# Attention block on one core: first x block in two transfers and four pieces, first K and Q from unpadded weights, first score tiles by head pairs, some bound rows on GpSimd

## The chip, the cores and the metric

The kernel runs on one core of one Trainium2 chip. The metric is device time in microseconds (us), the median of three runs. A core has a matrix engine (TensorE, here PE, with its weight loads shown apart as PEld), a vector engine (VectorE, DVE), an engine for functions such as the exponential (ScalarE, ACT), a programmable one (GpSimd, POOL) and an engine that issues transfers (SyncE, SP). Each takes its own instructions in the order in which the program lists them and waits on semaphores for what others have to finish. Matmul results go to PSUM, everything else lives in SBUF, and 16 DMA engines move data between these and DRAM.

## The reference

One attention block in bfloat16: a sequence of 2048 rows of 448 columns, 16 heads of 28 columns each. The scale is 28 to the power of -1/2.

```python
def reference(x, wqkv, wo):
    B, S, D = x.shape                      # 1, 2048, 448
    H = 16
    Dh = D // H                            # 28
    qkv = (x @ wqkv).reshape(B, S, 3, H, Dh).transpose(2, 0, 3, 1, 4)
    q, k, v = qkv[0], qkv[1], qkv[2]
    scores = jnp.einsum("bhqd,bhkd->bhqk", q, k) * (Dh ** -0.5)
    p = softmax(scores, axis=-1)
    o = jnp.einsum("bhqk,bhkd->bhqd", p, v)
    return o.transpose(0, 2, 1, 3).reshape(B, S, D) @ wo
```

## The kernel before

**Tiling.** The 16 heads are taken in four groups of four (G, HG), the 2048 queries in four chunks of 512 (QW), the 2048 keys in 16 tiles of 128. A window is one group with one chunk of queries; there are 16. A score tile is 128 keys by 512 queries of one head, 1024 in all: one matmul (L874) into a PSUM bank. A head has 28 columns and is padded to 32 partitions (HP), so four heads lie side by side on 128 partitions. Two heads share a 64-row matmul operand: KB[.][0] and QB[.][0] serve heads 0 and 1 of a group, KB[.][1] and QB[.][1] heads 2 and 3.

**Softmax with a bound.** In place of a row maximum an upper bound of each score is subtracted by the score matmul itself. Of the 64 rows of an operand, 32 carry a head's K or Q, and the other 32 carry bound rows: on the Q side the absolute values of Q times the K maxima (L681 to L691), on the K side a negative constant. For key block 0 and the first two windows the constants come from bndcol in the eviction (L547). For key blocks 1 to 3 they are the ratio of the maximum over all keys (KMAX, L580) to that over block 0 (RK0, L545), written into NK (L585) and copied out by DMA (L600). Four to eight DMAs (L590) move K itself to its place.

**Exponentials.** Most score tiles go in pairs through a two-bank PSUM slot (PA) to ACT (L1294, 128x1024). The others go one at a time through PD: DVE and POOL compute the exponential from a polynomial in the bits (L1075, L1078, L1081, L1094), and a few tiles do it almost wholly on POOL (L1007 to L1037). The value matmuls (L1139) add up four heads at once in PO.

**Order.** All of it stands in one function. The code first lists operations with an engine, an assumed duration, dependencies and a priority (class Op, add), then runs a small event simulation of the five engines (L1339 to L1392) and emits the instructions in the order that this simulation chose. The numbers in the operations are assumptions that decide an order; on the chip each engine just follows that order and the semaphores. A changed assumption such as XLAT, the assumed landing times of the x blocks, can therefore reorder the whole program.

**The start.** SP issues the first x block, the Q weights, two more x blocks and the V weights (L281 to L288), then four transposing loads of the last x block (L291). ACT issues the K weights (L280) and loads its function table (L297). PE runs eight filler matmuls on zeros (L404), then transposes x block 0 in two halves of eight (L425). DVE evicts the first half and half of the second, ACT the other (L436, L438). The weights of the first group are copied into padded form by DVE and ACT (L389, L390). K and Q of block 0 are four matmuls each with 112 rows per step (L531, L661). ACT evicts Q (L675) and K twice (L547), DVE reduces K's maximum (L538), forms the bound rows (L681 to L687) and evicts the later x blocks, with ACT taking one half (L438). Then the first scores follow.

**Order of the first score tiles.** `tile_of` maps the running number of a tile to its window, key tile and head. Within a row of four tiles all heads of one key tile come first:

```python
def tile_of(n):
    k, i = divmod(n, HG)
    w, j = row_of(k)
    g, c = divmod(w, NQC)
    return w, g, c, j, i
```

The first two windows run over the first four key tiles (FB) each, before the rest of either.

Of the kernel before, what the change touches and what calls it, by code (L numbers as in the profile page):

```python
# [9 lines left out]
ACT = mybir.ActivationFunctionType  # L10
ALU = mybir.AluOpType
# [7 lines left out]
P = 128  # L19
# [65 lines left out]
def kernel(  # L85
# [91 lines left out]
    XLAT = (4.6, 7.3, 8.9, 9.6)  # L177
# [11 lines left out]
    WQE = 'ACT'  # L189
    QORD = 0  # L190
    KCH = ((1, 2), (2, 4))
    RCH = ((1, 4), (0, 1))
# [3 lines left out]
    HENG = ('ACT', 'ACT', 'DVE', 'DVE')  # L196
# [188 lines left out]
    def pad_w(W, WP, g, eng):  # L385
        o = WP[g][:].rearrange("p c (h e) -> p c h e", e=HP)[:, :, :, 0:Dh]
        i = W[:, :, g * GW:(g + 1) * GW].rearrange("p c (h d) -> p c h d", d=Dh)
        if eng == "DVE":
            return lambda: nc.vector.tensor_copy(out=o, in_=i)  # L389
        return lambda: nc.scalar.copy(out=o, in_=i)  # L390
# [3 lines left out]
    xsp = []  # L394
# [3 lines left out]
    tbank = (((PD[0][:], None), (PD[1][:], None)), ((PD[2][:], None), (PA[0][:, 0:QW], None)),  # L398
             ((PO[:], None), (PD[1][:], -2)), ((PD[2][:], 2), (PO[:], 3)))
# [10 lines left out]
    for b in range(NQC - XBAR):  # L410
        xs_in = add(Op("SP", 0.01, None, prio=-2000 + b, lat=XLAT[b]))
        for hf in range(2):
            tv = tbank[b][hf][0].bitcast(BF16)

            if b == 0 and hf == 1 and XSP:
                tv2 = PA[0][:, QW:2 * QW].bitcast(BF16)
            else:
                tv2 = tv
# [8 lines left out]
            tro = add(Op("PE", 0.55 if b else (0.75, 0.65)[hf], tr, deps=[xs_in], prio=(-1200 if b else -5000) + 10 * b + (hf ^ THF[b]), lat=PLAT, kind="T",  # L427
                         elig=None if 2 * b + hf < 2 + TE else lambda t: len(k0mm) == 2 * CC and all(o.end is not None for o in k0mm),
# [10 lines left out]
            if b == 0 and hf == 1 and XSP:  # L439
                evo = add(Op("ACT", 0.48, lambda ev=ev: ev(eng="ACT", c1=1), deps=[tro], prio=-4999))  # L440
                xt_done[b].append(evo)
                evo = add(Op("DVE", 0.36, lambda ev=ev: ev(eng="DVE", c0=1), deps=[tro], prio=-4999))
                xsp.append(evo)
            else:
                evo = add(Op(eng, 0.655 if eng == "DVE" else 0.905, ev, deps=[tro], prio=(EVP[b] if b else -5000) + 10 * b + hf,
                             elig=None if b == 0 or eng == 'ACT' or not BW[b] else lambda t, b=b: len(qb0) == HG and qb0[BW[b] - 1].end is not None))
# [28 lines left out]
    for (W, WP, nm, win) in ((WK, WKP, "k", wkin), (WQ, WQP, "q", wqin)):  # L475
        eng = "DVE" if nm == "k" else WQE
        w_ready[(nm, 0)] = add(Op(eng, 0.3 if eng == "DVE" else 0.45, pad_w(W, WP, 0, eng), deps=[win], prio=-5001 + (nm == "q") * 2.5))
# [27 lines left out]
    def chain_mm(n, fn, deps, prio, elig, acq, half=None):  # L505
        ops = []
        for k in range(n):
            o = add(Op("PE", MM, (lambda k=k: fn(k)), deps=deps if k == 0 else [ops[-1]] + (half if half and k == 2 else []),
                       prio=prio + (0.001 if half is None else 10) * k, kind="B",
                       elig=elig, acq=acq if k == 0 else None, lat=0.0 if k < n - 1 else PLAT))  # L510
            ops.append(o)
        return ops

    k0_bank = [PD[0][:], PD[0][:], PD[1][:], PO[:]]
    k0_wait = [lambda: [xt_half[0]], lambda: kuse[0], lambda: [xt_half[5]], lambda: [xt_half[4]]]

    def task_K(g, sc):
# [11 lines left out]
        def ap():  # L529
            return task["ap"] if "ap" in task else bank(task)[:]  # L530
        ops = chain_mm(CC, lambda cc: nc.tensor.matmul(out=ap(), lhsT=WKP[g][:, cc, :], rhs=XT[sc][cc // 2][0:CK, cc % 2, :],  # L531
                                                       start=(cc == 0), stop=(cc == CC - 1)),
                       (xt_done[sc] if g or sc else xt_done[0][:1]) + [w_ready[("k", g)]], prio, elig, acq, half=None if g or sc else xt_done[0][1:])
        if g == 0 and sc == 0:
            k0mm.extend(ops)
        cs = slice(sc * QW, (sc + 1) * QW)
# [39 lines left out]
    def task_kmax(g):  # L576
# [7 lines left out]
        if g == 0:  # L584
            nk = add(Op("DVE", 0.2, lambda: nc.vector.tensor_scalar(  # L585
                out=NK[0][:], in0=maskm[:, 0:P], scalar1=KMAX[0][:, 0:1], scalar2=RK0[:, 0:1], op0=ALU.mult, op1=ALU.mult),
                deps=[m] + rk_op, prio=prio + 0.2))
# [48 lines left out]
    def task_Q(g, c):  # L636
# [4 lines left out]
        if w == 0:  # L641
            task = {"slot": d_slots[1]}
            acq = lambda t: xt_half[1].done(t)
            elig = None
            prio = -4500
        else:
# [9 lines left out]
            elif w == NF:  # L656
# [4 lines left out]
        ops = chain_mm(CC, lambda cc: nc.tensor.matmul(out=ap(), lhsT=WQP[g][:, cc, :], rhs=XT[c][cc // 2][0:CK, cc % 2, :],  # L661
                                                       start=(cc == 0), stop=(cc == CC - 1)),
                       (xt_done[c] if w else xt_done[0][:1]) + [w_ready[("q", g)]], prio, elig, acq, half=None if w else xt_done[0][1:])
# [8 lines left out]
        if w < NF:  # L672
            pq = -4390 if w == 0 else Q1P - 900
            if w == 0:
                e0 = add(Op("ACT", 0.62, lambda: nc.scalar.activation(  # L675
                    out=qb[0][:], in_=ap(), func=ACT.Identity, bias=offscol[:, 0:1], scale=YSC), deps=[ops[-1]], prio=pq, lat=0.17))
                quse.extend([e0])
# [5 lines left out]
            e1 = add(Op("DVE", TS5, lambda: nc.vector.tensor_copy(out=qb[1][:], in_=qb[0][:]), deps=[e0], prio=pq + 15))  # L683

            def bound(q, i, col, deps, prio):
                st = SI[i]
                return add(Op("DVE", 0.36, lambda: nc.vector.tensor_scalar(  # L687
                    out=q[i // 2][HP * (st ^ 1):HP * ((st ^ 1) + 1), :], in0=QP[n][HP * st:HP * (st + 1), :],
                    scalar1=col[HP * st:HP * (st + 1), 0:1], scalar2=None, op0=ALU.mult), deps=deps, prio=prio))
            for i in range(HG):  # L690
                o = bound(qb, i, KPART[0], [ab, kmaxop[0][0], e1], pq + (20 if i < 2 else 40) + 0.01 * i)  # L691
# [74 lines left out]
    open_when(a_slots[0], [xt_half[3]])  # L766
    a_slots[1].free_at = 0.0
# [97 lines left out]
    def tile_of(n):  # L865
        k, i = divmod(n, HG)
        w, j = row_of(k)
# [595 lines left out]
```

## Time and profile before

| what | value |
|---|---|
| three runs | 410.1, 410.3, 410.46 us |
| median | 410.3 us |
| profiled execution, its own time | 410.69 us |
| its span in the profile | 408.5 us |
| granted TensorE clock, mean | 1.00 |
| ACT, exponentials (L1294) | 422 of them, 388.0 us summed |
| first exponential starts, last one ends | 11.35 and 400.45 us |
| DMA in the first 10 us | 16 to 310 GB/s in steps of 2 us |

A line of a timeline gives the start, the duration from the first start to the last end, the engine, the source line, the operation, output and inputs with shapes, and how many were merged. In square brackets stands how long the engine was idle before it, and what released it. A line of groups gives the summed time, the mean of one in ns, and the idle time before. Consecutive instructions of an engine overlap a little, so that sums of durations can exceed the time that passed.

### The profile page before, as it was taken

To read this page: it belongs to the slowest core of one execution; us is meant where nothing else is said; L and a number is where in the kernel's file an instruction comes from. 1 tells how busy PE (TensorE), PEld (TensorE's weight loads), DVE (VectorE), ACT (ScalarE), POOL (GpSimd) and SP (SyncE) were. 2 spreads that over 40 slices of the span, in tenths; PEclk is the share of its full clock that TensorE was granted. 3 is DMA by queue.
4 is the path that set the end of the run, shared out by engine and by line. 5 is a ranking of instruction groups with operands and counts; after the bars stand their busy time and mean duration, and the time that the engine had idled before them with its cause. 6 is when DMAs were issued, how large, how long until landed. Compare 5 with 4: busy or idle time off the path is not lost.

```text
span 408.5 us, 7585 instructions
## 1 busy us (share of the span) xinstructions
PE 358.8 (88%) x2595; PEld 120.7 (30%) x2606; DVE 380.7 (93%) x664; ACT 395.5 (97%) x434; POOL 341.0 (83%) x365
## 2 busy tenths in 40 slices
PE   8999988998888989888897989889788888889896
PEld 5343232322223232322322232232222222222222
DVE  5996999999899999999989999999989999998983
ACT  4999999999999999999999999999999999999994
POOL 5049998899898999989899998979979989989950
PEclk9999999999999999999999999999999999999999
DMA  9353031112301020200500001000330001010121
GB/s 208 56 85 81 3 57 43 19 47 52 61 3 53 19 41 19 43 2 10 127 18 30 22 7 47 4 30 21 67 64 6 26 11 42 2 52 2 45 103 66
DMA packets 36871, 17.30 MB, mean 42 GB/s; under 512 B 29217, under 2 KB 33569, under 8 KB 36833
## 3 DMA queue, kind: packets, MB, share of 16 engines
q1 hardware_dynamic: 36224, 16.61, 17.8%
q8 instruction: 20, 0.33, 0.3%
q10 hardware_dynamic: 608, 0.22, 0.2%
q14 instruction: 19, 0.15, 0.1%
HBM read 6.91 MB, written 2.33 MB: 23 GB/s over the span
## 4 chain that ended last, share of the span: by engine, by line
ACT 43%; DVE 34%; PE 10%; issue 6%; POOL 4%; DMA 1%; DVEq 0%; SPq 0%; POOLq 0%; ACTq 0%
ACT PTA L1294 43%; DVE DU L1075 8%; DVE DV L1078 8%; DVE PTD L1094 8%; PE PA L874 3%; PE PO L1139 3%; POOL DG L1081 2%; DVE KB L566 1%; DVE SG L1007 1%; PE PD L874 1%; DVE KPART L570 1%; DVE VA L748 1%; DMA RRB<-SCR 1%; PE PA L404 1%; DVE DRC L968 1%
## 5 line engine op out<-in xcount | busy, mean ns | idle before, releaser
L1294 ACT ACTIVATE PTA<-PA 128x1024 bf16<-128x1024 f32 x422 | 388.0, 1175 | 0.9 <-PE PA L874 0.4
L1081 POOL TENSOR_TENSOR DG<-DV,DU 128x512 f16<-128x512 f16 x155 | 177.4, 1154 | 34.2 <-DVE DV L1078 29.8
L874 PE MATMUL PA<-QB,KB 64*128 64x512 bf16 x843 | 169.1, 380 | 36.4 <-ACT PTA L1294 33.6
L874 PEld LDWEIGHTS <-KB 64*128 64x128 bf16 x1024 | 65.4, 93 | 177.9 <-issue 169.3
L1094 DVE SCALAR_TENSOR_TENSOR PTD<-PD,DG 128x512 uint16<-128x512 f32 x155 | 104.7, 682 | 8.2 <-POOL DG L1081 7.8
L1075 DVE TENSOR_SCALAR DU<-PD 128x512 f16<-128x512 uint16 x155 | 103.6, 681 | 5.1 <-PE PD L874 4.8
L1078 DVE SCALAR_TENSOR_TENSOR DV<-PD,DU 128x512 f16<-128x512 uint16 x155 | 103.6, 682 | 0.8
L1139 PE MATMUL PO<-PTA,VA 128*32 128x512 bf16 x843 | 85.5, 386 | 0.7 <-DVE QB L671 0.4
L874 PE MATMUL PD<-QB,KB 64*128 64x512 bf16 x181 | 66.3, 377 | 5.0 <-DVE PTD L1094 3.3
L1139 PE MATMUL PO<-PTD,VA 128*32 128x512 bf16 x181 | 55.6, 386 | 0.3
L1139 PEld LDWEIGHTS <-VA 128*32 128x32 bf16 x1024 | 19.9, 94 | 50.0 <-issue 48.7
L1024 POOL TENSOR_TENSOR SG<-SG,GU 128x512 f32<-128x512 f32 x26 | 30.0, 1156 | 3.0 <-DVE QP L700 2.1
L1022 POOL TENSOR_TENSOR GU<-GV,GU 128x512 f16<-128x512 f16 x26 | 30.0, 1155 | 2.0 <-DVE QP L700 1.4
L1020 POOL TENSOR_TENSOR GV<-GE,GU 128x512 f16<-128x512 f32 x26 | 30.1, 1157 | 1.4
L974 POOL TENSOR_TENSOR OT<-OSB,RRB 128x512 bf16<-128x512 f32 x15 | 19.0, 1269 | 5.2 <-DMA RRB<-SCR 3.7
L1014 POOL TENSOR_SCALAR GU<-SG 128x512 f16<-128x512 uint16 x26 | 16.1, 617 | 5.5 <-DVE SG L1007 3.1
L1007 DVE COPY SG<-PD 128x512 f32<-128x512 f32 x26 | 17.8, 683 | 2.2 <-PE PD L874 2.0
L661 PE MATMUL PO<-XT,WQP 112*128 112x512 bf16 x56 | 18.7, 386 | 0.5 <-DVE KB L558 0.4
L1017 POOL TENSOR_SCALAR GE<-SG 128x512 f32<-128x512 uint16 x26 | 16.1, 618 | 2.9 <-DVE QP L700 1.0
L1037 POOL TENSOR_SCALAR PTD<-SG 128x512 uint16<-128x512 f32 x26 | 16.1, 619 | 1.9 <-DVE KPART L570 0.5
L732 PEld LDWEIGHTS <-XT 112*128 112x128 bf16 x256 | 13.6, 98 | 10.5 <-issue 10.2
L531 PE MATMUL PO<-XT,WKP 112*128 112x512 bf16 x48 | 15.5, 385 | 0.4 <-DVE OSB L959 0.4
(109 smaller groups left out, 201.7 us busy)
## 6 DMA issues: line engine op xcount, KB each, us to landing
RRB<-SCR SPq DMA_DIRECT2D x15, 256.0 KB, 3.3
QB<-QP SPq DMA_DIRECT2D x56, 32.0 KB, 1.8
KB<-NK SPq DMA_DIRECT2D x12, 128.0 KB, 3.0
XS<-in_x_dram SPq DMA_DIRECT2D x3, 448.0 KB, 5.8
QB<-QB SPq DMA_DIRECT2D x28, 32.0 KB, 1.8
out_dram<-XS SPq DMA_DIRECT2D x2, 448.0 KB, 2.5
KB<-KB SPq DMA_DIRECT2D x6, 128.0 KB, 2.3
RRB<-RR SPq DMA_DIRECT2D x2, 256.0 KB, 3.4
```

What stands on the lines that cost most here:

```text
L874: nc.tensor.matmul(out=ap, lhsT=KB[g % 2][i // 2][a:a + 64, j * P:(j + 1) * P], rhs=QB[w % NQB][i // 2][a:a + 64, :], start=True, stop=Tru ...
L974: o5 = add(Op("POOL", 1.22, lambda: nc.gpsimd.tensor_tensor(out=OT[g][c][:], in0=OSB[b][:], in1=RRB[b][:], op=ALU.mult), deps=o4, prio=-10 ...
L1007: cp = add(Op("DVE", CPY, lambda: nc.vector.tensor_copy(out=X[:], in_=PX[slot.idx][:]), deps=[sop], prio=n - O1))
L1020: g3 = add(Op("POOL", PTT, lambda: nc.gpsimd.tensor_tensor(out=GV[:], in0=GE[:], in1=GU[:], op=ALU.mult), deps=[g2], prio=prio + 2, kind=" ...
L1022: g4 = add(Op("POOL", PTT, lambda: nc.gpsimd.tensor_tensor(out=GU[:], in0=GV[:], in1=GU[:], op=ALU.mult), deps=[g3], prio=prio + 3, kind=" ...
L1024: g5 = add(Op("POOL", PST, lambda: nc.gpsimd.tensor_tensor(out=X[:], in0=X[:], in1=GU[:], op=ALU.add), deps=[g4], prio=prio + 4, kind="g", ...
L1075: p1 = add(Op("DVE", P1, lambda: nc.vector.tensor_scalar(out=DU[b][:], in0=lo, scalar1=SIG / 65536, scalar2=SIG * (SS - 0.5), op0=ALU.mult ...
L1078: p2 = add(Op("DVE", P1, lambda: nc.vector.scalar_tensor_tensor(out=DV[b][:], in0=lo, scalar=65536 * (SS - 0.5 + CE / C3), in1=DU[b][:], o ...
L1081: gq = add(Op("POOL", PTT, lambda: nc.gpsimd.tensor_tensor(out=DG[b][:], in0=DV[b][:], in1=DU[b][:], op=ALU.mult), deps=[p2], prio=n, kind ...
L1094: f = add(Op("DVE", P1, lambda: nc.vector.scalar_tensor_tensor(out=PTD[st["s"].idx][:].bitcast(U16), in0=PX[slot.idx][:], scalar=EBITS + C ...
L1139: nc.tensor.matmul(out=PO[HP * st:HP * (st + 1), :], lhsT=VA[g][:, j, st, :], rhs=r["p"][i][1](), start=first, stop=last, tile_position=(0 ...
L1294: nc.scalar.activation(out=PTA[pslot.idx][:, 0:len(ns) * QW], in_=PA[s.idx][:, 0:len(ns) * QW], func=ACT.Exp, bias=ACT_BIAS, scale=ACT_SCALE)
```

## The change

- **First x block.** It is loaded as two transfers of 224 KB, one on SP's queue and one on ACT's, behind the K weights. Its 16 transposes come as two groups of eight, one for each transfer, into four banks (t0_bank); each of the four pieces of 112 columns is evicted by itself, ACT and DVE in turn.
- **First K and Q.** For group 0 and block 0 the matmuls read WK and WQ as they were loaded: one matmul for each head and step, 28 columns wide, at its own column position (strips_mm), into a bank that a matmul of zeros cleared. Q comes before K at each step. The padded copies, which the later blocks read, are made on POOL.
- **Evictions.** ACT evicts Q of window 0 twice in place of a DVE copy. The second half of x block 1 goes from ACT to DVE.
- **Bound rows.** For heads 2 and 3 of the first two windows, and for key block 1, POOL computes the bound rows; the DMAs from NK then cover key blocks 2 and 3 only. RK0 is multiplied by KMAX in an instruction of its own.
- **Score order.** In the first two windows eight tiles of heads 0 and 1 (four key tiles) come before the eight of heads 2 and 3.
- **Fillers.** Four filler matmuls in place of eight, and the twelve optional ones between 4.6 and 9 us of the simulation are gone.
- **Order.** Assumed times and priorities are changed, so the order of instructions differs from the start on. In the built program 844 score tiles go to ACT (843 before) in 422 instructions, all of them full (before, one of the 422 held a single tile); 25 tiles (26) take the way that is almost wholly POOL's.

```diff
-    XLAT = (4.6, 7.3, 8.9, 9.6)
+    XLAT = (None, 6.5, 8.8, 9.6)
...
+    NWARM = 4
+    XLAT0 = (4.0, 4.8)
...
-    RCH = ((1, 4), (0, 1))
+    RCH = ((2, 4), (0, 1))
...
-    HENG = ('ACT', 'ACT', 'DVE', 'DVE')
+    HENG = ('ACT', 'DVE', 'DVE', 'DVE')
...
-        if b < NQC - 1:
+        if b == 0:
+            for h, q in ((0, nc.sync), (1, nc.scalar)):
+                ts = slice(h * TPC // 2, (h + 1) * TPC // 2)
+                q.dma_start(out=XS[0][:, ts, :], in_=x_perm[:, ts, :])
+        elif b < NQC - 1:
...
+        return lambda: nc.gpsimd.tensor_copy(out=o, in_=i)
...
-    for n in range(8):
+    for n in range(NWARM):
...
-    for n in range(12):
-        add(Op("PE", MM, lambda: warm(n), prio=5000, kind="K", elig=lambda t: 4.6 < t < 9, acq=lambda t: warm_open[0]))
...
+    xt0 = []
+    t0_bank = (PO[:], PA[1][:, 0:QW], PA[0][:, 0:QW], PA[0][:, QW:2 * QW])
...
+    for h in range(2):
+        for cc in range(CC):
+            def tr(h=h, cc=cc):
+                for t in range(h * TPC // 2, (h + 1) * TPC // 2):
+                    nc.tensor.transpose(out=t0_bank[cc].bitcast(BF16)[0:CK, t * P:(t + 1) * P],
+                                        in_=XS[0][:, t, cc * CK:(cc + 1) * CK], identity=ident[:])
...
+    for cc in range(CC):
+        eng = ("ACT", "DVE")[cc % 2]
+
+        def ev0(cc=cc, eng=eng):
+            (nc.scalar.copy if eng == "ACT" else nc.vector.tensor_copy)(
+                out=XT[0][cc // 2][:, cc % 2, :], in_=t0_bank[cc].bitcast(BF16)[0:CK, 0:QW])
...
+    def strips_mm(bank, W, win, prio):
+        ops = []
+
+        def clear():
+            nc.tensor.matmul(out=bank, lhsT=zeros[:], rhs=zrow[:], start=True, stop=False, skip_group_check=True)
+        z = add(Op("PE", 2 * MM, clear, deps=[z_in], prio=-5100, kind="K", lat=0.0))
+        for cc in range(CC):
+            def mm(cc=cc):
+                for h in range(HG):
+                    nc.tensor.matmul(out=bank[HP * h:HP * h + Dh, :], lhsT=W[:, cc, h * Dh:(h + 1) * Dh], rhs=XT[0][cc // 2][0:CK, cc % 2, :],
+                                     start=False, stop=(cc == CC - 1), tile_position=(0, HP * h), skip_group_check=True)
...
+            kr = add(Op("DVE", 0.07, lambda: nc.vector.tensor_scalar(
+                out=RK0[:], in0=KMAX[0][:], scalar1=RK0[:, 0:1], scalar2=None, op0=ALU.mult), deps=[m] + rk_op, prio=prio + 0.2))
+            for i in range(HG):
+                def rows0(i=i):
+                    st = SI[i]
+                    nc.gpsimd.tensor_scalar(out=KB[0][i // 2][HP * (st ^ 1):HP * ((st ^ 1) + 1), QW:2 * QW], in0=maskm[HP * st:HP * (st + 1), :],
+                                            scalar1=RK0[HP * st:HP * (st + 1), 0:1], scalar2=0.0, op0=ALU.mult, op1=ALU.add)
...
+                e1 = add(Op("ACT", 0.62, lambda: nc.scalar.activation(
+                    out=qb[1][:], in_=ap(), func=ACT.Identity, bias=offscol[:, 0:1], scale=YSC), deps=[ops[-1]], prio=pq + 15, lat=0.17))
...
+                if i < 2:
+                    return add(Op("DVE", 0.36, lambda: nc.vector.tensor_scalar(out=o, in0=q, scalar1=km, scalar2=None, op0=ALU.mult), deps=deps, prio=prio))
+                return add(Op("POOL", 0.6, lambda: nc.gpsimd.tensor_scalar(out=o, in0=q, scalar1=km, scalar2=0.0, op0=ALU.mult, op1=ALU.add),
+                              deps=deps, prio=prio))
...
+        if k < FB * NF:
+            k, r = divmod(n, FB * HG)
+            k, i = k * FB + r % (2 * FB) // 2, r // (2 * FB) * 2 + r % 2
```

More of the change, by code (lines that the diff above doesn't have):

```diff
@@ L413 @@
             tv = tbank[b][hf][0].bitcast(BF16)
[L415 to L418, printed above, removed]
+            tv2 = tv
             def tr(b=b, hf=hf, tv=tv, tv2=tv2):
@@ L438, in ev @@
                     nc.scalar.copy(out=XT[b][hf][:, c0:c1, :], in_=i)
[L439 to L446, printed above, removed]
+            evo = add(Op(eng, 0.655 if eng == "DVE" else 0.905, ev, deps=[tro], prio=EVP[b] + 10 * b + hf,
+                         elig=None if eng == 'ACT' or not BW[b] else lambda t, b=b: len(qb0) == HG and qb0[BW[b] - 1].end is not None))
             xt_done[b].append(evo)
@@ L765 @@
     task_Q(0, 0)
-    open_when(a_slots[0], [xt_half[3]])
-    a_slots[1].free_at = 0.0
+    for s in a_slots:
+        s.free_at = 0.0
     open_when(d_slots[0], kuse[1])
```

74 lines of the change are left out of this document (40 added, 34 removed).

## The prediction

> **What bounds the kernel now.** I read the engine totals and the costliest groups first, then the timelines of the first 22 us and of the last 15 us, since the diff touches the start and what the new order leaves at the end.
>
> ```profile
> PE 358.8 (88%) x2595; PEld 120.7 (30%) x2606; DVE 380.7 (93%) x664; ACT 395.5 (97%) x434; POOL 341.0 (83%) x365
> ...
> L1294 ACT ACTIVATE PTA<-PA 128x1024 bf16<-128x1024 f32 x422 | 388.0, 1175 | 0.9 <-PE PA L874 0.4
> ```
>
> ACT is busy 97% of the span, and in its 422 exponentials it waited 0.9 us in all. They run without a real gap from the first one at 11.35 to the end of the last at 400.45. So every us by which the first starts earlier is a us at the end, as long as PE keeps them fed; work taken from DVE, POOL or SP later is worth nothing by itself. What sets the first exponential stands in the ACT timeline:
>
> ```profile
> 8.53 0.69 ACT L675 ACTIVATE QB<-PD,offscol 128x512 bf16<-128x512 f32 x1 [1.67 <-PE PD L661]
> 9.12 0.77 ACT L547 ACTIVATE KB<-PD,bndcol,selcol 128x512 bf16<-128x512 f32 x1
> 9.78 1.01 ACT L438 COPY XT<-PA 112x1024 bf16<-112x1024 bf16 x1
> 10.67 0.80 ACT L547 ACTIVATE KB<-PD,bndcol,selcol 128x512 bf16<-128x512 f32 x1
> 11.35 18.91 ACT L1294 ACTIVATE PTA<-PA 128x1024 bf16<-128x1024 f32 x20
> ```
>
> ACT goes without a gap from the first Q eviction (8.53) to the first exponential: four steps (0.59, 0.66, 0.89, 0.68 from start to start), 2.82 us. Beside it run PE and DVE:
>
> ```profile
> 1.26 3.57 PE L404 MATMUL PA<-zrow,zeros 128*128 128x512 bf16 x8 [1.26 <-DVE zrow L302]
> 4.71 1.53 PE L425 MATMUL PD<-ident,XS 128*112 128x128 bf16 x12
> ...
> 6.59 0.61 PE L531 MATMUL PD<-XT,WKP 112*128 112x512 bf16 x2
> ...
> 7.68 0.81 PE L661 MATMUL PD<-XT,WQP 112*128 112x512 bf16 x3
> ...
> 9.61 0.65 PE L425 MATMUL PO<-ident,XS 128*112 128x128 bf16 x8 [0.22 <-DMA XS<-in_x_dram]
> 10.10 0.61 PE L425 MATMUL PD<-ident,XS 128*112 128x128 bf16 x8
> 10.64 0.39 PE L874 MATMUL PA<-QB,KB 64*128 64x512 bf16 x2
> ```
>
> The first x block lands 3.9 us after its issue at 0.74; PE transposes it from 4.71, K and Q end at 7.84 and 8.49, and the first scores (10.64) follow DVE's bound rows (9.78 to 10.50). The third block, XS2, lands only at about 9.57. The reader should also see two speeds: the eight matmuls of 512 columns at 1.26 start 0.43 us apart and the transposes 0.107, while from 6.59 on matmuls start 0.215 apart and transposes 0.055. Yet the granted clock reads 1.00 in every stage.
>
> **The change, part by part.** Times below are worked out from these rows.
>
> First x block. Its first half comes on SP's queue as before, its second on ACT's, behind WK. WK was issued at 0.74 and landed after 4.2, at 4.94. The DMA engines are 95 to 102% busy from 2 to 8 us, so the second half cannot be there before the whole block was, 4.64; served only after WK, its 224 KB at the 310 GB/s of the window 4 to 6 take 0.74 more, 5.68. I take 5.0, since nearly all of WK's packets had moved by 4 us and half as much now competes with them. The eight transposes left then start at 5.07, the last at 5.82; each result is readable 0.35 after its start. ACT evicts piece 0 at 5.55 to 6.14 (0.59, the row at 6.27) and piece 2 at 6.2 to 6.79; DVE's piece 3 waits in the built program for ACT's piece 2, so 6.85 to 7.27 (0.42).
>
> K and Q. Four narrow matmuls side by side cost what one wide one does: on the chain of waits L1139's last 36 take 2.11 us, or (2.11 - 0.38) / 35 = 0.05 each, 0.2 for four. So eight steps of 0.215 from 6.18, 0.04 after piece 0 is evicted: Q ends at 7.86 (before 8.49), K at 8.08 (7.84). The weight copies (DVE 0.48, ACT 0.57) leave for POOL; each was done by 6.07, so this frees nothing on the path. POOL has no such row: 0.62 (a 128x512 L1014) to 1.29 (its memset) each, both done by 8.1, while the padded weights are first read after the second score pair, past 10.5; without this cover PE's next Q would wait as long.
>
> ACT then runs Q, Q again (replacing DVE's 0.29 copy), K, K from 7.9: 0.59, 0.59, 0.66, 0.68, free at 10.43. The 1.01 copy is gone to DVE, behind the bound rows there. DVE: reduce 8.12 to 8.81, absolute value 8.85, maximum 9.06, two bound rows 9.38 to 10.10 (all at the spacing of before). The other two go to POOL, for the fifth exponential four us later: hidden at 0.62 or 1.29 each. PE has the first eight XS2 transposes queued ahead of the first scores: 9.57, plus 0.04 and 0.49, gives 10.10 and binds no earlier than DVE. Scores at 10.24 (0.14 after the rows, as 10.50 to 10.64), exponential at 10.24 + 0.39 + 0.04 = **10.67, 0.68 earlier** (0.39 is the pair's row; 0.04 lies between Q's end at 8.49 and ACT's 8.53). If the half lands at 4.64, XS2 still holds the scores at 10.12 (gain 0.80); at 5.68 the gain is nil.
>
> Head pairs. Eight tiles of one head pair now precede eight of the other, so the pair evicted last is first needed by the fifth exponential instead of the second. But in the built order the last K piece follows the eleventh score pair, where it followed the seventh. A pair goes out about 0.63 us before its exponential, at a cadence of 0.928 (the first 25, 11.35 to 34.56); the eleventh at 19.3, K done 19.98, reduced 20.7, maximum 20.83, one K eviction, scaled maximum 21.55. NK was ready at 20.41 before.
>
> Bound rows of block 1. POOL writes four from 21.7. No row has a 32-partition operation that moves between partitions; by L1014's 0.62 at 0.69 spacing they end at 24.45, by L1081's two-input 1.15 at 26.3. The pair that needs rows 3 and 4 is the 17th, at 24.9: covered by 0.4 with 0.69, the nearest operation. The K moves (L590, 0.65 apart, 2.1 to land) end by 22.1, before 24.0. SP's later rows and moves end by 29.1 against 30.4. SP's second to fourth transposing loads now wait for WK and the halves; these issue at 5.31 to 9.44, and the latest half is there at 5.68.
>
> End.
>
> ```profile
> 398.80 1.65 ACT L1294 ACTIVATE PTA<-PA 128x1024 bf16<-128x1024 f32 x2
> ...
> 400.50 1.03 PE L1139 MATMUL PO<-PTA,VA 128*32 128x512 bf16 x13
> ...
> 401.60 0.72 DVE L886 STREAM_TRANSPOSE SG<-PO 128x512 f32<-128x512 f32 x1 [2.23 <-PE PO L1139]
> ```
>
> ACT gets 844 score tiles instead of 843: the last exponential is full, +0.44 (1176 against 740 ns). After the last scores 28 value matmuls remain instead of 36, 8 x 0.05 = 0.4 less, but a projection eviction (0.61) now stands on DVE just ahead of the final transpose and waits for a matmul put before the last four. Instead of 1.15 after the last exponential the transpose starts 0.65 to 1.15 after it; I take 0.95 (that matmul's 0.36 and the eviction's 0.61, one after the other), **-0.20**.
>
> Sum: -0.68 + 0.44 - 0.20 = **-0.44**. The profiled execution took 410.69 with a span of 408.5 and 2.2 around it, so it would take 410.25; it lies 0.39 over the median 410.3, which becomes **409.86**.
>
> **Rivals.** *A: PE is still slow for K and Q.* The filler matmuls at the start fall from eight to four, and twelve optional ones go. Two bank clears and four fillers end at 3.84, then PE has only transposes and gaps until 6.18. If full speed had come with the steady work, these eight steps run at 0.43: K ends at 9.8, reduce 10.5, bound rows 11.84, first exponential 12.4. +1.06 + 0.44 - 0.20 = +1.30, **411.6**: slower. It outweighs the gain from two slow steps (2 x 0.215 = 0.43) on. For it: in before the fast rows begin only after 5.3 us of unbroken work. Against: transposes are work of PE too, and they filled 4.7 to 6.5 there. [...]
>
> *B: POOL's rows cost 1.15.* The 17th pair waits until 26.35 instead of 24.9: +1.45, **411.3**. For it: partition shift; against: one input, like L1014.
>
> *C: the transfers help more.* XS2 lands by 9.2, the second half at 4.6; first exponential 10.27, and the end gains the 0.5 of its better bound: -1.08 + 0.44 - 0.50 = -1.14, **409.2**. For it: SP's queue is shorter by 224 KB; against: the same bytes on busy engines.
>
> *D: the split brings nothing.* Half lands at 5.68, the end gains nothing: +0.44, **410.7**.
>
> **How the numbers follow.** Forecast 0.36 (its own range 409.4 to 410.3), C 0.24, D 0.16, A 0.16, B 0.08. 0.2% is 0.82 us, about what a measurement here can tell: faster means under 409.5. That holds in nearly all of C (0.22) and the forecast's lower end (0.11), 0.33; slower means over 411.1, most of A and B (0.22) and a little of D on top of a slow step (0.02), 0.24; the same 0.43. The range runs from just under C, 409.0, to near A, 411.5.
>
> **What would show it.** First exponential at 10.5 to 10.8; the second half's first transposes at about 5.0; Q and K steps 0.215 apart (0.43 is A); first scores right behind DVE's bound rows or XS2's transposes; no ACT gap between 20 and 32 us (a gap of over 1 us behind POOL's rows at about 25 is B); the final DVE transpose about 0.95 after the last exponential. A first exponential after 11.1, or ACT gaps of over 0.5 us later on, makes the prediction wrong.

## The result, and the profile after

The changed kernel takes 409.0 us (median of 6 runs, 408.47 to 409.21) where the kernel before took 410.42 beside it (6 runs, 410.1 to 411.28): a ratio of 0.996, 95% interval 0.9947 to 0.9973, so 1.4 us faster. The forecast was 409.86. Its sign was right and its size too small: 0.44 us forecast against 1.42 between the medians (410.69 to 408.98 between the two profiled executions).

The engine totals and the line of the exponentials, of the changed kernel (busy us, mean ns of one, then idle time ahead of them):

```profile
PE 358.5 (88%) x2611; PEld 119.8 (29%) x2621; DVE 379.2 (93%) x659; ACT 395.3 (97%) x434; POOL 341.9 (84%) x369
...
L1337 ACT ACTIVATE PTA<-PA 128x1024 bf16<-128x1024 f32 x422 | 388.2, 1162 | 0.7 <-PE PA L917 0.6
```

These look like before: 422 exponentials, 388 us, under 1 us of idle time. The ACT timeline of the start, from the first Q eviction on (start, duration, engine, operation):

```profile
7.95 0.69 ACT L709 ACTIVATE QB<-PD,offscol 128x512 bf16<-128x512 f32 x1 [1.30 <-PE PD L534]
8.54 0.68 ACT L711 ACTIVATE QB<-PD,offscol 128x512 bf16<-128x512 f32 x1
9.11 1.45 ACT L571 ACTIVATE KB<-PD,bndcol,selcol 128x512 bf16<-128x512 f32 x2
10.69 20.27 ACT L1337 ACTIVATE PTA<-PA 128x1024 bf16<-128x1024 f32 x22
```

The first exponential starts at 10.69, against 11.35 before and 10.67 forecast. Q is evicted from 7.95 instead of 8.53; from there to the first exponential it takes 2.74 us instead of 2.82. PE's own start, and lines from the timelines of DVE and POOL:

```profile
3.96 0.46 PE L418 MATMUL PO<-ident,XS 128*112 128x128 bf16 x2
4.21 0.85 PE L418 MATMUL PA<-ident,XS 128*112 128x128 bf16 x6
5.17 0.37 PE L418 MATMUL PO<-ident,XS 128*112 128x128 bf16 x2
5.38 0.50 PE L418 MATMUL PA<-ident,XS 128*112 128x128 bf16 x6
6.21 0.40 PE L534 MATMUL PD<-XT,WQ 112*28 112x512 bf16 x4 [0.34 <-ACT XT L425]
6.43 0.40 PE L534 MATMUL PD<-XT,WK 112*28 112x512 bf16 x4
```

```profile
9.16 1.06 DVE L727 TENSOR_SCALAR QB<-QP,KPART 32x512 bf16<-32x512 bf16 x2
```

```profile
9.39 1.47 POOL L728 TENSOR_SCALAR QB<-QP,KPART 32x512 bf16<-32x512 bf16 x2 [3.43 <-ACT QB L711]
...
21.67 3.01 POOL L614 TENSOR_SCALAR KB<-maskm,RK 32x512 bf16<-32x512 bf16 x4 [3.02 <-DVE RK L609]
```

The halves of the x block are there at 3.92 and 5.12 (from issue to landing 3.2 and 3.9); four narrow matmuls are one step of 0.215. DVE's two bound rows take 1.06 together, where two took 0.72 before (L687 at 9.78). POOL's four rows of block 1 end at 24.68. The end, from the timeline of all engines:

```profile
397.62 1.97 ACT L1337 ACTIVATE PTA<-PA 128x1024 bf16<-128x1024 f32 x2
...
399.53 0.36 PE L951 MATMUL PD<-WO,OT 128*128 128x448 bf16 x1
...
399.82 0.40 PE L1182 MATMUL PO<-PTA,VA 128*32 128x512 bf16 x4
...
400.28 0.72 DVE L929 STREAM_TRANSPOSE SG<-PO 128x512 f32<-128x512 f32 x1 [2.62 <-PE PO L1182]
```

The last exponential ends at 399.58, and the final transpose starts 0.70 later (1.15 before).

Where the 1.3 us of span went, between the profiled executions: the first exponential is 0.66 earlier; from the start of the first to the start of the last exponential it takes 387.83 instead of 388.36, -0.53; the last one lasts 1.06 instead of 0.74, +0.32; behind it 7.65 us are left instead of 8.10, -0.45. Another 0.39 lies outside the span (2.14 became 1.75). Over all runs it is 1.73 on average in the 6 runs of the changed kernel, and 2.04 in the 23 of the kernel before that ran beside the second set of experiments. The five parts add up to 1.71, the difference of the two profiled executions; the medians are 1.42 apart.

So a half of the gain was not where the forecast looked. The -0.53 is the puzzle: a stage in which, by the page, ACT hardly waits became shorter. The starts of single exponentials show two things that the page hides.

The first is the spacing itself. More than half of the exponentials start at most 0.907 after the one before, and these intervals average 0.9042 in the profiled execution of the kernel before and 0.9034 in that of the changed kernel. Over 421 intervals this makes 0.34 of the 0.53. It is no work of the edit: experiment 5 below, in the changed kernel's own order, has 0.9042, and experiments 6 to 8, in the same order, have 0.9034. No run says where the two values come from.

The second is waits. Over 421 times this spacing, the stage is longer by 7.7 us before and 7.5 after, a difference of 0.18. The page shows only 0.9 and 0.7 as idle, because an exponential that starts on time is shown with up to 1.31 us (1.29 in the changed kernel) and overlaps the next, while one that was waited for is shown with about 1.02: most of a wait only shortens the overlap. 29 of the intervals before, and 29 after, are longer than 0.96; they hold 5.6 and 5.9 us. (One of them, 1.38 in both, is an instruction of ACT's own between two exponentials, L935 and L978.) One such place in the changed kernel, with the exponential that came late last:

```profile
66.71 0.69 DVE L1137 SCALAR_TENSOR_TENSOR PTD<-PD,DG 128x512 uint16<-128x512 f32 x1 [0.73 <-POOL DG L1124]
...
67.46 0.37 PE L917 MATMUL PD<-QB,KB 64*128 64x512 bf16 x1 [0.56 <-DVE PTD L1137]
...
67.76 0.40 PE L1182 MATMUL PO<-PTA,VA 128*32 128x512 bf16 x3
...
68.09 0.39 PE L917 MATMUL PA<-QB,KB 64*128 64x512 bf16 x2
...
68.58 1.02 ACT L1337 ACTIVATE PTA<-PA 128x1024 bf16<-128x1024 f32 x1 [0.40 <-PE PA L917]
```

DVE waited for POOL, PE's next score tile (into PD) waited for DVE, and the pair that ACT needed stood behind it in PE's queue. This interval was 1.46, of which the bracket shows 0.40. Which places become so is mostly decided by the order that the planner laid out, as experiment 12 shows, and the change altered that order nearly everywhere behind the start. But the sum of the waits changed by less than it differs between executions of one order: in experiments 5 to 8, all in the changed kernel's order, it is 7.3 to 8.1 us, around the 7.7 of the kernel before.

### The profile page after: what moved, and what is told of

It reads as the page before. It is cut to its first block, busy times and chain, and to the rows that moved or that the text cites. A ratio compares the mean times of both kernels' runs of the same rounds, so it can differ in the third digit from the quotient of the medians.

```text
span 407.2 us, 7611 instructions
## 1 busy us (share of the span) xinstructions
PE 358.5 (88%) x2611; PEld 119.8 (29%) x2621; DVE 379.2 (93%) x659; ACT 395.3 (97%) x434; POOL 341.9 (84%) x369
## 4 chain that ended last, share of the span: by engine, by line
ACT 43%; DVE 22%; PE 11%; POOL 10%; issue 7%; DMA 4%; SPq 1%; ACTq 0%; DVEq 0%; POOLq 0%
ACT PTA L1337 43%; DVE PTD L1137 6%; DVE DU L1118 5%; POOL DG L1124 5%; DVE DV L1121 5%; PE PA L917 4%; PE PO L1182 3%; DMA RRB<-SCR 2%; PE PD L917 1%; POOL SG L1067 1%; POOL GV L1063 1%; SPq L464 1%; DMA XS<-in_x_dram 1%; DVE SG L1050 1%; DMA RRB<-RR 1%
## 5 line engine op out<-in xcount | busy, mean ns | idle before, releaser
L1063 POOL TENSOR_TENSOR GV<-GE,GU 128x512 f16<-128x512 f32 x25 | 28.9, 1156 | 2.7 <-DVE QP L740 1.7
L1067 POOL TENSOR_TENSOR SG<-SG,GU 128x512 f32<-128x512 f32 x25 | 28.9, 1155 | 1.8 <-DVE QP L740 1.0
L1065 POOL TENSOR_TENSOR GU<-GV,GU 128x512 f16<-128x512 f16 x25 | 28.8, 1154 | 1.2 <-DVE DRC L1011 0.5
L557 PE MATMUL PO<-XT,WKP 112*128 112x512 bf16 x52 | 17.2, 384 | 0.7 <-DVE QB L705 0.3
```

Source lines behind the costliest of these rows:

```text
L1063: g3 = add(Op("POOL", PTT, lambda: nc.gpsimd.tensor_tensor(out=GV[:], in0=GE[:], in1=GU[:], op=ALU.mult), deps=[g2], prio=prio + 2, kind=" ...
L1065: g4 = add(Op("POOL", PTT, lambda: nc.gpsimd.tensor_tensor(out=GU[:], in0=GV[:], in1=GU[:], op=ALU.mult), deps=[g3], prio=prio + 3, kind=" ...
L1067: g5 = add(Op("POOL", PST, lambda: nc.gpsimd.tensor_tensor(out=X[:], in0=X[:], in1=GU[:], op=ALU.add), deps=[g4], prio=prio + 4, kind="g", ...
```

## The experiments

Two theories stood against each other. **Theory 1**: the earlier start (0.66) is the change's own work and carries to the end one for one; the rest is the order of all that follows, which any edit of the plan throws anew, with -1 to +3 us. **Theory 2**: the change itself, by its head pairs and by the rows moved to POOL, makes the exponentials denser.

### One constant of the planner, in both kernels

Experiments 1 and 4 change the lookahead, 2 and 3 the order in which POOL's path takes the heads; nothing of the change is touched.

```diff
-    LA = 10
+    LA = 11
```

```diff
-    GI = (3, 1, 2, 0)
+    GI = (2, 1, 3, 0)
```

The kernel before with the new lookahead:

> The kernel before with one constant of the order changed (LA 10 to 11: how far ahead a tile is taken for POOL). The first 41 exponentials and all that stands ahead of them keep their order; later on the order differs, and 12 value matmuls stand behind the last score instead of 36. Theory 1 (the gain has three parts: the start, 0.66 us; the order in which the rest happens to be laid out, 0.5 us; the end, 0.4 us, by what is left behind the last score): first exponential at 11.35 as before, but the time leaves 410.4 by 0.3 us or more, to either side, with nothing of the change in it; the end behind the last exponential under 7.75 us (8.05 before). Theory 2 (the change itself, its head pairs and its POOL rows, makes the 422 exponentials denser, and the end goes with it): within 0.2 us of before.

The kernel before with the new order of heads:

> The kernel before with another constant changed (GI: which head's tile POOL takes first). The order differs from the 40th exponential on, 16 value matmuls stand behind the last score. Theory 1: first exponential 11.35; the stage of the exponentials moves by some tenths either way, the end is under 7.75 us, the time differs from 410.4 and from the run with LA. Theory 2: within 0.2 us of before.

The changed kernel with the new order of heads:

> The changed kernel with the same edit of GI: order different from the 39th exponential on, 846 score tiles on ACT (one exponential more), 8 value matmuls behind the last score. Theory 1: first exponential at 10.69; the time moves off 409.0 by 0.3 us or more, the likely side is later since ACT has 0.9 us more to do. Theory 2: 409.0 plus the 0.9 of one more exponential at most, and as dense as in the changed kernel (0.921 from start to start).

The changed kernel with the new lookahead:

> The changed kernel with LA 11: order different from the 39th exponential on, 843 score tiles on ACT as before (421 full and a half one), 32 value matmuls behind the last score. Theory 1: first exponential 10.69; mean distance of the exponentials anywhere between 0.919 and 0.925; the time within 1 us of 409.0 but not on it. Theory 2: 0.921 from start to start, 408.6 by the half exponential less.

Measured, each against the kernel before on the same chip (first exponential and first-to-last start from one profiled execution each):

| kernel | median us | ratio, 95% interval | first exponential | first to last start |
|---|---|---|---|---|
| before, LA 11 | 408.75 | 0.9977 (0.9964 to 0.9990) | 11.32 | 386.82 |
| before, GI | 409.72 | 1.0001 (0.9992 to 1.0010) | 11.98 | 388.15 |
| changed, GI | 412.12 | 1.0057 (1.0045 to 1.0069) | 10.76 | 390.70 |
| changed, LA 11 | 412.39 | 1.0071 (1.0058 to 1.0084) | 10.60 | 391.30 |

With LA 11 the median of the kernel before falls by 1.24 us against the runs beside it, without any of the change (by the ratio, 0.23% against the change's 0.4%), and the changed kernel loses all of its gain and 2.4 us more. Theory 2 falls as a rule about density, and theory 1 holds in the main: the stage spans 386.8 to 391.3 with no tie to the change. (Experiment 3 has one exponential more in it, 0.9 us.) Not all came as theory 1 had it. Experiment 2 is within theory 2's 0.2 us of the kernel before, and its end is 7.93 instead of under 7.75; experiment 4 was to stay within 1 us of 409.0.

The start stays earlier with the change in each pair: 0.72 with LA 11, 1.22 with GI. The larger number has a cause of its own. In the profiled execution of experiment 2, K begins at 7.24 instead of 6.59. From its timelines of POOL and DVE:

```profile
5.21 1.25 POOL L459 MEMSET VA<- 128x256 bf16 x1
```

```profile
5.26 1.34 DVE L389 COPY WKP<-WK 112x448 bf16<-112x448 bf16 x1 [0.77 <-DMA WK<-in_wqkv_dram]
```

And the same copy in the kernel before:

```profile
5.25 0.48 DVE L389 COPY WKP<-WK 112x448 bf16<-112x448 bf16 x1 [0.77 <-DMA WK<-in_wqkv_dram]
```

DVE's copy of the K weights took 1.34 instead of 0.48. In the kernel before, that memset of POOL's starts only at 5.64; in this execution it was 0.04 ahead of the copy. DVE then evicts the first x block at 6.52 instead of 5.84, and so K is late (0.13 of it is a later landing of that block). The runs of experiment 2 fall in two groups, seven at 409.64 to 409.79 and four, the profiled one among them, at 410.47 to 410.72. The change moves these copies to POOL and so does away with this meeting of copy and memset; how often it befalls the kernel before itself, and so how much of the 1.42 it makes, no run shows.

### Parts of the start, under a held order

In the next four, the planned order of every engine is the changed kernel's.

**Experiment 5: the split of the first x block.** One transfer on SP's queue again.

```diff
-            for h, q in ((0, nc.sync), (1, nc.scalar)):
-                ts = slice(h * TPC // 2, (h + 1) * TPC // 2)
-                q.dma_start(out=XS[0][:, ts, :], in_=x_perm[:, ts, :])
+            nc.sync.dma_start(out=XS[0][:], in_=x_perm[:, 0:TPC, :])
```

> The changed kernel with the first x block in one transfer on SP's queue, as before; the planned order of every engine is held, so that only the start can differ. Split helps: all 16 transposes begin at about 4.7 (before: 4.71) instead of 3.96 and 5.17, at 0.07 to 0.107 each they end at 5.8 to 6.4 instead of 5.7, K and Q begin at 6.3 to 6.7, the first exponential is 0.1 to 0.5 later than 10.69. Split brings nothing (rival D): first exponential within 0.1 of 10.69. Either way, if the start carries to the end one for one under a held order (theory 1), the last exponential and the time move by the same amount, 0 to +0.5 us on 409.0; if the density of the exponentials is a lottery even under a held order, they move by something else.

Its twelve executions fall in two groups, seven at 408.48 to 409.49 and five at 410.01 to 411.29 (median 409.41, ratio 0.9987, interval 0.9972 to 1.0002). The profiled one took the longest. From its PE timeline:

```profile
4.55 0.46 PE L416 MATMUL PO<-ident,XS 128*112 128x128 bf16 x2 [0.58 <-DMA XS<-in_x_dram]
...
6.54 0.61 PE L532 MATMUL PD<-XT,WQ 112*28 112x512 bf16 x4
6.92 0.66 PE L532 MATMUL PD<-XT,WK 112*28 112x512 bf16 x4
7.34 0.66 PE L532 MATMUL PD<-XT,WQ 112*28 112x512 bf16 x4
```

The expectation missed what mattered. K and Q begin 0.33 later, as expected, but their steps are 0.43 apart: PE, idle for 0.58 ahead of the block, was at half speed until 10.6. The first exponential comes at 12.69, 2.0 late, and that execution is 2.3 slower than the changed kernel's. That the group at about 409 had PE at full speed is inferred from its times; none of it was profiled. If so, the split gains little in transfer time, and what it buys is that PE has transposes to do from 3.96 instead of a pause.

**Experiment 6: the fillers.** Four filler matmuls left out; they compute nothing that is used.

```diff
-        add(Op("PE", 2 * MM, lambda: warm(n), deps=[z_in], prio=-3000 + n, kind="K"))
+        add(Op("PE", 2 * MM, None, deps=[z_in], prio=-3000 + n, kind="K"))
```

> The changed kernel without its four filler matmuls at the start (they compute nothing that is used); planned order held. Clock theory (rival A's mechanism): PE has then only two bank clears before the first block lands, stays at half speed, the transposes are 0.107 apart and the eight K and Q steps 0.43 (some of them at least): first exponential 11.1 to 12.8 and the time up by the same 0.4 to 2.1 us, 409.4 to 411.1. Without a clock that depends on earlier work: steps stay 0.215, first exponential 10.7, time 409.0.

```profile
6.22 0.62 PE L534 MATMUL PD<-XT,WQ 112*28 112x512 bf16 x4
6.60 0.67 PE L534 MATMUL PD<-XT,WK 112*28 112x512 bf16 x4
...
8.30 0.60 PE L534 MATMUL PD<-XT,WK 112*28 112x512 bf16 x4
8.72 0.40 PE L534 MATMUL PD<-XT,WQ 112*28 112x512 bf16 x4
8.94 0.39 PE L534 MATMUL PD<-XT,WK 112*28 112x512 bf16 x4
```

Without the fillers rival A's slow steps come: five of about 0.43 (6.60 to 8.72), 0.215 only from 8.7, the first exponential at 11.89, and 410.33 us (ratio 1.0007, interval 0.9998 to 1.0016). This also measures how a start carries: the first exponential is 1.21 later than the changed kernel's, the last one ends 1.01 later, and the time is 1.18 to 1.29 above the two kernels beside it (409.15 and 409.04).

**Experiment 7: the unpadded weights.** K and Q from the padded copies, one 128-column matmul per step:

```diff
-                for h in range(HG):
-                    nc.tensor.matmul(out=bank[HP * h:HP * h + Dh, :], lhsT=W[:, cc, h * Dh:(h + 1) * Dh], ...
+                nc.tensor.matmul(out=bank, lhsT=WP[:, cc, :], rhs=XT[0][cc // 2][0:CK, cc % 2, :],
```

> The changed kernel with the first K and Q made from the padded weights again, one 128-column matmul per step instead of four of 28; GpSimd still makes the copies, ahead of them; the rest of the order held. If the unpadded weights save a wait: GpSimd's two copies end at about 5.2 and 6.0, in time for K's steps or not by a few tenths, so K and Q begin 0 to 0.3 later and the first exponential is 10.7 to 11.0. If four narrow matmuls cost more than one wide one: steps below 0.215 and a first exponential before 10.6. Forecast's own step (0.2 for four narrow ones, copies hidden): first exponential within 0.1 of 10.69, time 409.0.

```profile
4.65 0.56 POOL L398 COPY WKP<-WK 112x448 bf16<-112x448 bf16 x1
5.27 0.56 POOL L398 COPY WQP<-WQ 112x448 bf16<-112x448 bf16 x1
```

The copies are done at 5.83, before the first step at 6.19; steps stay 0.215, the first exponential comes at 10.63, the time is 409.04 (0.9968, interval 0.9956 to 0.9980). Unpadded weights save nothing here, and four narrow matmuls cost what one wide one does, as the prediction had it.

**Experiment 8: POOL's rows kept off DVE's.** POOL's two bound rows of the first window wait until DVE has written its two.

```diff
+                        r = nc.vector.tensor_scalar(out=o, in0=q, scalar1=km, scalar2=None, op0=ALU.mult)
+                        if w == 0:
+                            row2.append(r)
+                            if len(row2) == 2:
+                                for f in late:
+                                    tc.add_manual_dep(f().ins, r.ins.name, sync)
```

> The changed kernel, in which GpSimd's two bound rows of the first block wait until VectorE has written its own two; planned order held. If GpSimd's row slows VectorE's second one (0.69 instead of 0.34 beside it): VectorE's second row takes 0.34 again, the first scores go out at about 9.9 for both heads and the first exponential starts 0.2 to 0.35 before 10.69; GpSimd's rows end at about 11 instead of 10.86, still before the fifth exponential (14.3) needs them; time 408.7 if the start carries. If the 0.69 belongs to that row itself: it stays 0.69 and nothing moves.

```profile
8.96 0.72 DVE L730 TENSOR_SCALAR QB<-QP,KPART 32x512 bf16<-32x512 bf16 x2
```

DVE's two rows take 0.72 again, in this run and in three later ones with the same edit, against 1.06 in the changed kernel; the second row cost 0.34 more for POOL's company. The first exponential is at 10.23, 0.46 earlier, of which 0.20 is a first K and Q step at 6.01 in this execution. The time does not show it: 409.15 (0.9970, interval 0.9958 to 0.9982). In the profiled execution two neighbouring intervals near 356 us are 1.48 long. The window around them (its length, busy time of PE, PEld, DVE, ACT and POOL, then the granted clock):

```profile
356.00:359.00 3.00, 3.00 (x10) 0.47 (x8) 1.99 (x5) 2.44 (x3) 2.39 (x3) 0.50 0.05 11
```

For 3 us PE got half its clock, which cost 2 x (1.48 - 0.90) = 1.15. Without that this execution would have taken about 408.0, an estimate. The other four, with a mean granted clock of 0.999 or 1.00, took 408.46 to 409.84, so the estimate is not borne out. Their starts were not profiled; whether the 0.3 reaches the time stays open.

### Other orders

**Experiment 9: the first score tiles head by head again.** The three lines added to `tile_of` are taken out; the plan is made anew.

> The changed kernel with the first score tiles in the order of before (head by head); the order of the engines is planned anew for it and differs from the changed kernel's in what stands around the 31st exponential and later. Head pairs matter for the start: the second score tile pair now needs GpSimd's two bound rows (10.86) and waits, an ACT gap of 0.3 to 0.6 after the first exponential. Head pairs matter for nothing else (theory 1): behind that, the time between exponentials is that of a new laid-out order, -1 to +3 us on 387.8 from first to last start, whatever the tiles; under theory 2 (the head pairs make the exponentials denser) the stage goes back to 388.4 or more because of them and the time to 409.5 to 410.4.

408.95 us (0.9957, interval 0.9942 to 0.9972). The expected wait did not come: the first exponential is at 10.60 and the next ones follow without a gap. POOL's rows end at 10.8 and their pair is due at 11.5, so the "fifth exponential" was never needed as cover. The stage takes 387.61. Head pairs bring nothing at the start. Behind it the order is another one too, so that a small effect of theirs could not be told from the order's.

**Experiments 10 to 12: three more constants, each with POOL's rows held back as above:** J0 10 to 11, GBEG 40 to 60, J3 9 to 10. (J0 and J3 are how many tiles must be ready before the value matmuls of a window begin, J3 for the last four windows; the first of the next expectations describes J0 wrongly.)

> The changed kernel with GpSimd's two bound rows held back as before (first exponential 10.2 to 10.5) and one constant of the planner changed (J0, how many of a row's tiles go to the exponential before one is given to the other path, 10 to 11): 841 tiles instead of 844, same order up to the 57th exponential. Theory 1: long intervals repeat at the same places, 25, 36, 45 to 56, with the same length within 0.1, and are at other places and of another sum behind the 57th; stage 386.8 to 391, time 408 to 412, not to be told beforehand.

> The same held-back rows with another constant of the planner changed (GBEG, from which tile GpSimd's path begins, 40 to 60): 844 tiles, same order up to the 22nd exponential. Theory 1: another sum, places of the long intervals differ from the 22nd on; stage 386.8 to 391, time 408 to 412.

> The same held-back rows with a constant that moves only the last quarter (J3, 9 to 10): 843 tiles, the order of every score tile is the changed kernel's up to the 360th exponential. Theory 1: at least 20 of its 25 long intervals (over 0.96) up to the 355th stand at the changed kernel's own places, with the same length within 0.1, and the sum of what lies over 0.904 up to the 336th interval is within 0.6 of 5.9; behind the 360th they differ; last exponential 0.4 shorter. If the long intervals belong to the execution instead of the order, fewer than 10 repeat. First exponential 10.2 to 10.5; if that start carries, time 408.0 to 409.0.

| kernel | median us | ratio, 95% interval | first exponential | first to last start | last exponential's end to final transpose |
|---|---|---|---|---|---|
| J0 11 | 412.74 | 1.0053 (1.0033 to 1.0072) | 10.37 | 393.11 | 0.61 |
| GBEG 60 | 408.61 | 0.9957 (0.9944 to 0.9971) | 10.69 | 387.31 | 0.70 |
| J3 10 | 411.7 | 1.0036 (1.0019 to 1.0052) | 10.80 | 388.04 | 2.68 |

The third is the sharp test. Its order equals the changed kernel's up to the 360th exponential, and 24 of the changed kernel's 25 long intervals up to the 355th stand at the same places, within 0.1 us; one more appears; the sum over the first 336 intervals is 6.05 against 5.91. With GBEG, whose order parts at the 22nd exponential, 1 of 29 repeats. So most of the long intervals belong to the order, not to the execution. Two expectations failed besides. J0's stage and time lie outside what was expected. And with GBEG and J3 the first exponential was to come at 10.2 to 10.5: DVE's two rows did take 0.72, but the first K and Q step with GBEG, and the first two with J3, were still slow (0.38, and 0.38 and 0.33 to the next start), and DVE's reduction of K began at 8.43 and 8.45 instead of 8.17.

J0 turns one place into a wait of its own:

```profile
70.83 1.94 ACT L1349 ACTIVATE PTA<-PA 128x1024 bf16<-128x1024 f32 x2 [4.78 <-PE PO L1194]
```

The mean granted clock of this execution is 0.992, against 1.00 in the changed kernel's; how much of the wait is PE's clock, the mean does not tell.

J3 leaves the stage as it is and loses 2.0 us at the end. From its DVE timeline there:

```profile
401.66 0.62 DVE L872 TENSOR_TENSOR XS<-PD,KB 128x448 bf16<-128x448 f32 x1 [2.65 <-PE PD L868]
402.20 0.71 DVE L941 STREAM_TRANSPOSE SG<-PO 128x512 f32<-128x512 f32 x1
```

A projection eviction stands in DVE's queue ahead of the final transpose and waits 2.65 us for PE, though the last value matmuls were through at about 400.2.

GBEG 60 with the rows held back has the lowest median at 408.61, and the kernel before with LA 11 is at 408.75, on another chip. GBEG 60 is faster than the kernel before, but its interval covers the changed kernel's ratio: no version here is shown to beat the changed kernel.

## Why the prediction was right, and where it failed

**The start: right, with two small errors that nearly cancel.** The second half of x landed at 5.12 (5.0 forecast), K and Q began at 6.21 (6.18) in steps of 0.215, Q's eviction at 7.95 (7.9), the first exponential at 10.69 (10.67). Inside that, DVE's bound rows began 0.22 earlier than forecast, since the reciprocal had gone behind them, and took 0.34 longer, since POOL wrote its own beside them; that POOL's two rows would be "hidden" at any length overlooked that one of them, beside DVE's second row, could lengthen it: 0.69 there, and 0.34 alone. That a later start carries to the end is shown by experiments 5 and 6; the earlier start of experiment 8 was not seen in its time.

**Rival A: right to be priced.** It did not come in the profiled execution, but the margin was small, and that it did not is in part luck: without the four fillers it is measured at +1.3, with one transfer it came in the profiled execution, and with fillers and split in place experiments 11 and 12 still had one and two slow steps. The prediction's "two slow steps" that outweigh the gain were that near.

**Head pairs, unpadded weights, block 1's rows: right that they cost nothing on the path.** POOL's rows took 0.75 each instead of 0.69 and ended at 24.68 against 24.45, with no ACT gap, so rival B falls. Experiments 7 and 9 show that the first two bring nothing at the start either. That moving the weight copies "frees nothing on the path" holds for the execution that the prediction read; experiment 2 shows one in which DVE's copy held up K by 0.65.

**Rival C: nearest in time, not in mechanism.** Its 409.2 needed a first exponential at 10.27. XS2 did land by 9.2, at 8.73 instead of 9.56, but the second half of the first block came at 5.12 and not by 4.6. XS2's transposes then waited for ACT's second Q eviction, which frees their bank (9.27), and DVE's rows set the start.

**The failed step: "They run without a real gap", and with it a stage put at nothing.** Between the profiled executions the forecast missed 1.27 us (1.71 against 0.44): 0.53 in this stage, 0.39 outside the span, 0.25 at the end and 0.12 in the last exponential. The prediction read 0.9 us of idle time as the whole of what ACT waits, and so kept the stage unchanged while the diff re-laid the order of the whole program. The intervals hold over 7 us of waits, the order mostly decides where they fall, and orders that differ in one constant moved the stage by -1.5 to +5.3, the last in an execution with a mean granted clock of 0.992. The term was 0; it measured -0.53. Of that, 0.34 is the spacing of one execution against that of another, and the 0.18 of waits is within what one order shows from execution to execution. So the reason given for the 0 was wrong, and its honest range was a few us in both directions, wider than the prediction's whole own range of 409.4 to 410.3; but that the new order made the stage shorter is not shown, and what this stage adds to the gain between the medians stays open.

**The end: a term mis-sized, by a misread line.** The matmul just ahead of the last four value matmuls is L951, a late sum whose result DVE does not have to evict before the transpose; the projection eviction taken to wait for it (L860) was done at 397.65. So the transpose started 0.70 after the last exponential, near the bound of 0.65 that the prediction gave for it, and the term was -0.45 instead of -0.20. Experiment 12 shows the trap that the prediction feared, in another order, at 2.0 us. The last exponential's +0.44 was +0.32: the forecast took the mean of all, 1.176, and this one took 1.06.

**What lies around the span** was taken as a constant, 2.2, and so put at nothing; it went from 2.14 to 1.75 in the profiled executions. On average it is 1.71 to 1.73 in the changed kernel and in experiments 5 to 8, 2.02 to 2.06 in the kernel before on three chips, and up to 2.09 in other orders. No run says why. With it (0.31 on average), the start (0.66) and the end (0.45 less 0.32) the parts read from the profiles make 1.10 of the medians' 1.42.

## What to carry to other kernels

Where one engine runs back to back, look at the spacing of its starts instead of its idle time: waits can hide in the overlap of its records, and here over 6 of 7 us did. Compare the shortest spacing too: here two executions of one order differed by 0.34 us in it alone. If an edit makes a planner lay out the program anew, the new order is a term of its own, of either sign and as large as the edit; run a few orders of both kernels, or hold the order, before a gain is put down to the edit. Work that is taken from an engine's first microseconds can slow what follows, and is to be priced at the slow rate too: without its four fillers PE's K and Q steps were 0.43 apart until 8.7 instead of 0.215 (experiment 6).

## What the runs showed of the hardware

The moment at which PE's spacing halves moves from execution to execution. PE's first matmul starts at 1.26 in the changed kernel and in experiments 5 to 8, and the last filler at 3.34 or 3.35 in it and in experiments 7, 8, 11 and 12; 128-column transposes go from 0.107 to 0.056 apart at 4.1 in experiment 8 and at 5.3 in the changed kernel. In experiment 7 all sixteen, to 5.85, are slow and K and Q from 6.19 fast, and in experiments 11 and 12 the first steps of K and Q, from 6.30 and 6.22, are slow too, to 6.7 and 6.8: 2.9 to about 5.5 us after the start, with the same fillers. After the pause of 0.58 in experiment 5 it took 6.0 us from 4.55. The granted clock reads 1.00 in the starts of the kernel before and of the changed kernel, and 1.00 on average over the profiled executions of experiments 5 to 7, yet 0.50 in the slow 3 us at 356 in experiment 8. What sets the moment, no run shows.

A VectorE row of 32x512 bf16 takes 0.34 to 0.35 alone (eight of them in the kernel before). In the changed kernel it takes 0.69 (at 9.53) and 0.67 (at 16.04) beside a GpSimd row of the same shape; GpSimd's rows take 0.68 (at 9.39) and 0.76 (at 15.80) beside it, and the two behind these 0.69. A VectorE copy of 112x448 takes 0.48 in the kernel before, and 1.34 where a GpSimd memset of 1.25 began 0.04 before it (experiment 2). The copy ended 0.13 after the memset, less than its own 0.48, so a part of its work was done beside the memset. Why VectorE is slower beside GpSimd, no run shows.
